# Eight of a tile's 32 column blocks go from VectorE to ScalarE, in one stage of a decode block's forward and backward pass

## The chip, the cores and the metric

The kernel runs on one core of a Trainium2 chip. That core has five engines, each with an instruction queue of its own that is worked in order: TensorE (PE in the profile, its weight loads PEld), VectorE (DVE), ScalarE (ACT), GpSimd (POOL) and SyncE (SP). Transfers are issued from the queues of SP, POOL and ACT and are carried by 16 DMA engines. The metric is the time of one execution on the device in microseconds (us), the median of several runs.

## The reference

A block of a transformer for one decoded token: layer norm, attention over a cache of 4096 keys and values, a residual, layer norm, a two-layer MLP with ReLU, a residual. The batch B is 2, there are H = 32 heads of 128, and the model width D is 640. The kernel computes the output and the gradients for x, the key and value caches, and the four weight matrices.

```
q      = layernorm(x) @ wq
scores = q . k * 128**-0.5 ;  p = softmax(scores) ;  o = p . v        # per batch and head
h      = x + o @ wo
out    = h + relu(layernorm(h) @ w1) @ w2
grads  = vjp of out for (x, k_cache, v_cache, wq, wo, w1, w2)
```

What costs most is the two caches, 2 x 32 x 4096 x 128 in bf16 each (1 MB for a head of a batch), which are read, and their gradients of the same size, which are written. For one batch and head, with `go` the gradient of the head's output, the gradient of V is the outer product of p and `go`; that of K is the outer product of the scores' gradient p * (V . go - const) and q.

## The kernel before, in words

A head's tile of a cache lies in SBUF as 128 partitions x 32 column blocks of 128: partition p holds rows 32p to 32p + 31 of the sequence, one in each block. gV and gK have the same layout. The kernel writes its engines' instructions in an order fixed by hand (a manual schedule); python generators that are stepped in turn decide which instruction is written when.

**First pass** (`p1_iter`): for each of the 64 pairs of batch and head, scores, softmax weights (`P_bf`), and sums that the output and the gradient of q need. **Second pass** (`p2_iter`): for each pair, the products of V with `go`, then gV and gK. The plan runs the first pass of the first batch, then the rest of the first pass with second-pass turns between, and from the loop's index 66 on the second pass alone (`i is None`). The order of the second pass is `turns`; turns 0 to 31 are batch 0, 32 to 63 batch 1. Turns 14 to 64 run in the stage where the second pass is alone.

One turn j of `p2_iter`, in the order in which it is written:

1. PE does the last quarter of turn j - 1's matvec (L436, `pair_matvec` with T3); VectorE makes `gsp` of it (L821), the column factor for gK.
2. PE spreads two rows (L830); ScalarE scales them into `rb` (L835): columns 0 to 127 are the row factor of gV, 128 to 255 that of gK. POOL copies a column of `P_bf` doubled into `pp` (L837), the column factor of gV.
3. PE transposes the first quarter of the V tile (`Wt`) into one of two PSUM banks (L423), and ScalarE copies it out to `t_sb` (L428). VectorE makes gK of turn j - 1 in two halves (L808) and POOL issues its store (L846).
4. The other three quarters are transposed and copied out in the same way (T1, T2, T3), each matvec one step behind. After T3's transposes the V tile's buffer is given back, which lets SP issue a later load.
5. VectorE makes gV of turn j in two halves of 16 blocks (L808, called from `outer_half`), and POOL issues its store (L865).

Between these steps background generators are stepped, whose instructions land in the same queues: the middle of the layer (`middle_gen`: layer norms, the MLP, and the products with w1 and wo, L644 on VectorE), the outer products of the weights' gradients (`fin_gen`, with ScalarE copies `ot` at L908 and `wide`, `ar` and the like), and the gradient of x (`gx_gen`). `fin_gen` starts within turns 22 and 23.

gV and gK tiles take 1 MB buffers from a list with the tag `g` (five of them in this stage), and V tiles from one with the tag `ld`. A buffer of `g` is free again when its store has landed, so the engine that first writes the next tile in it waits for that landing.

Of the kernel before, what the change touches and what calls it, by code (L numbers as in the profile page):

```python
# [7 lines left out]
FP32 = mybir.dt.float32  # L8
BF16 = mybir.dt.bfloat16
ALU = mybir.AluOpType  # L10
ACT = mybir.ActivationFunctionType
# [4 lines left out]
def kernel(  # L16
# [20 lines left out]
    nc = tc.nc  # L37

    B, Sq, D = A_x.shape
    _, H, Sk, Dh = A_k_cache.shape  # L40
# [4 lines left out]
    NSC = Sk // 128  # L45
# [7 lines left out]
    HALF = NSC // 2  # L53
# [13 lines left out]
    small = ctx.enter_context(tc.tile_pool(name="small", bufs=3))  # L67
# [136 lines left out]
    P_bf = cols.tile([128, B * H, NSC], BF16)  # L204
# [210 lines left out]
    def pair_transpose(nat, g, dve=False, busy=0):  # L415


        t_ps = pst([128, GT // 2, 128], FP32, "tps", "t_ps")
        warm(t_ps[:].rearrange("p j k -> p (j k)"), nat, g, busy)
        natf = nat[:].bitcast(FP32)  # L420
        for j in range(GT // 2):
            cc = (g * GT) // 2 + j
            nc.tensor.transpose(t_ps[:, j, :], natf[:, 2 * cc:2 * cc + 2, :].rearrange("p c k -> p (c k)"), ident_f[:])  # L423
        t_sb = mats.tile([128, GT // 2, 128], FP32, tag="XT", bufs=5, name="t_sb")
        if dve:
            nc.vector.tensor_copy(out=t_sb[:], in_=t_ps[:])  # L426
        else:
            nc.scalar.copy(out=t_sb[:], in_=t_ps[:])  # L428
        return t_sb
# [373 lines left out]
    def pairs_view(t):  # L803
        return t.rearrange("p s (a two) -> p s a two", two=2)

    def outer_half(dst, row, colp, k):
        sl = slice(k * HALF, (k + 1) * HALF)
        nc.vector.tensor_tensor(  # L808
            out=pairs_view(dst[:, sl, :]),
            in0=row.rearrange("p (a two) -> p a two", two=2)[:, None, :, :].to_broadcast([128, HALF, 64, 2]),  # L810
            in1=colp[:, sl, None, :].to_broadcast([128, HALF, 64, 2]), op=ALU.mult)

    def p2_iter(j, busy):

        c = S2[j] if j < NP1 else None
        p = S2[j - 1] if j >= 1 else None
        if p is not None:
            bp, hp = turns[j - 1]
            pair_matvec(p["dp"], p.pop("T3"), 3, gom[:, hp, bp, :, :])
            gsp = small.tile([128, NSC, 2], BF16, tag="gsp", name="gsp")  # L820
            nc.vector.scalar_tensor_tensor(  # L821
                out=gsp[:], in0=p["dp"][:, :, None].to_broadcast([128, NSC, 2]), scalar=negdot[:, hp, bp:bp + 1],
                in1=P_bf[:, bp * H + hp, :, None].to_broadcast([128, NSC, 2]), op0=ALU.add, op1=ALU.mult)
        if c is not None:
            b, h = turns[j]
            go = gom[:, h, b, :, :]

            bank = pst([128, 512], FP32, "sps", "dp_ps")
            for k, col in enumerate((goc, qsc)):
                nc.tensor.matmul(bank[:, 128 + k * 128:256 + k * 128],  # L830
                                 lhsT=col[:, h, b:b + 1].to_broadcast([128, 128]), rhs=ident_bf[:],
                                 start=True, stop=True)
            c["dp"] = bank[:, 0:NSC]
            rb = mats.tile([128, 256], BF16, tag="rb", bufs=4, name="rb")
            nc.scalar.activation(out=rb[:], in_=bank[:, 128:384], func=ACT.Copy, scale=rt[:, b, h:h + 1])  # L835
            pp = small.tile([128, NSC, 2], BF16, tag="pp", name="pp")
            nc.gpsimd.tensor_copy(out=pp[:], in_=P_bf[:, b * H + h, :, None].to_broadcast([128, NSC, 2]))  # L837
            c.update(rb=rb, pp=pp)
            c["T0"] = pair_transpose(c["W"], 0, busy=busy)
        if p is not None:  # L840
            gK = take("g", [128, NSC, 128], "gK")
            outer_half(gK, p["rb"][:, 128:256], gsp, 0)
        yield
        if p is not None:
            outer_half(gK, p["rb"][:, 128:256], gsp, 1)
            nc.gpsimd.dma_start(out=natural(out_2, bp, hp), in_=gK[:])  # L846
            give(gK)
            del S2[j - 1]
        yield
        if c is None:  # L850
            return
        c["T1"] = pair_transpose(c["W"], 1, busy=busy)
        pair_matvec(c["dp"], c.pop("T0"), 0, go)
        yield
        c["T2"] = pair_transpose(c["W"], 2, busy=busy)
        pair_matvec(c["dp"], c.pop("T1"), 1, go)
        yield
        c["T3"] = pair_transpose(c["W"], 3, busy=busy)
        give(c["W"], "g" if j < H and j != 1 and owned["g"] < 3 else None)
        pair_matvec(c["dp"], c.pop("T2"), 2, go)  # L860
        gV = take("g", [128, NSC, 128], "gV")
        outer_half(gV, c["rb"][:, 0:128], c["pp"], 0)
        yield
        outer_half(gV, c["rb"][:, 0:128], c["pp"], 1)
        nc.gpsimd.dma_start(out=natural(out_3, b, h), in_=gV[:])  # L865
        give(gV)
        yield
# [213 lines left out]
    i = j = 0  # L1081
# [46 lines left out]
    g2 = None  # L1128
# [11 lines left out]
    for n, (i, j) in enumerate(plan):  # L1140
        all_go = all(("go", B - 1, h) in done for h in range(H))
        if i is None and plan[n - 1][0] is not None:
            pkp.release()
            big1 = tc.alloc_tile_pool(name="big1", bufs=1)
            for _ in range(2):
                more_home("ld", big1)
            share(ld=KEPT[1] + 4, g=5)
        if all_go and not late[0]:
            wop.release()
            big3 = tc.alloc_tile_pool(name="big3", bufs=1, side="right")  # L1150
            for tag in ("ld", "g", "g", "q", "q", "q"):
                more_home(tag, big3)
        late[0] = all_go
        more = int(late[0])
        if fin is not None and not bg2 and not bg3:
            share(ld=8 + 3 * more, g=7 + 3 * more)
        elif fin is not None and j >= H + KEPT[1] - 1:
            share(ld=5 + more, g=5 + 2 * more, f=3, q=2 + 3 * more)
        if j is not None:
            while g2 is not None:  # L1160
                p2_step()
            if j < NP1:
                bg_until(("go", *turns[j]))
            g2 = p2_iter(j, 0)
        if i is None and ("w1", 1) in done and fin is None:
            wts.release()
            fin = tc.alloc_tile_pool(name="fin", bufs=1)
            big2 = tc.alloc_tile_pool(name="big2", bufs=1)
            more_home("f", big2)
            banks.update(sps=[2, 3], o=[4, 5, 6])  # L1170
            bg2.append(("fin", fin_gen(fin)))
            bg3.append(("gx", gx_gen(fin)))
        if i == 12:
            bg.append(("ga", ga_gen()))
        if i == H + 2:
            banks["bc"].insert(0, banks["sps"].pop(0))
        elif i == P2_AT:
            banks["bc"].remove(7)
            banks["sps"].insert(0, banks["bc"][0])
            banks["bc"] = [7]  # L1180
        rate = RATES[0 if i is not None and i <= H + 1 else 1 if j is None and i < P2_AT else
                     2 if i is not None else 3 if j <= H else 4]
        if i is None:
            spread[0] = 2
            at_k[0] = 1
            k = 0
            while g2 is not None:
                p2_step()
                pump()
                slot[0] = int(k in ((1, 3, 5) if j <= H else (1, 4)))  # L1190
                k += 1
                bg_step(0, rate)
                bg_step(1, RATE2)
                bg_step(2, RATE3)
            continue
        at = MIXED if j is not None else REST
        for k, _ in enumerate(p1_iter(i, i < H + 1, 0)):
            for _ in range(at.get(k, 0)):
                if g2 is not None:
                    p2_step()  # L1200
            if k == 5:
                a_heads(i)
            pump()

            spread[0] = 1 if i < P2_AT else 2
            at_k[0] = k
            if i >= P2_AT:
                slot[0] = int(k == 6 or (k == 1 and j is None))
            elif i > H + 1:
                slot[0] = {1: 2, 3: 1, 4: 1, 6: 1}.get(k, 0)  # L1210
            else:
                slot[0] = int(k in (1, 6))
            bg_step(0, rate)
            bg_step(1, 0.0)
        if i is not None and i in (H + 1, NP1 + 1):
            bg.append((f"m{i // H - 1}", middle_gen(i // H - 1)))
# [41 lines left out]
```

## Time and profile before

| what | before |
|---|---|
| median of 3 runs | 903.56 us (903.27 to 903.65) |
| the profiled execution | 902.98 us, of which the span of instructions is 901.1 |
| PE, PEld busy | 739.2 us (82%), 618.0 us (69%) |
| DVE busy | 695.8 us (77%) |
| ACT busy | 442.9 us (49%) |
| POOL busy | 192.9 us (21%) |
| moved | 362.87 MB, 403 GB/s over the span |
| mean granted TensorE clock | 0.775 of full speed |

Busy time is summed over the whole span, and stages differ: a mean says little of one stage, which is why the prediction asks for windows. In the groups of instructions a line names its source line, engine, operation, output and input tiles with shapes and count, then busy time in us and the mean of one in ns, then idle time of that engine just before, with what ended it. In the chain of waits each piece has a start, a length and what the end of the span hung on at that time.

The stores of gV are issued by POOL at 483.74 us (turn 14), 519.00 (19), 552.28 (23), 586.48 (28) and 622.37 (32).

### The profile page before, as it was taken

The numbers are of one execution on the slowest core, as the hardware profiler recorded it, in microseconds if no ns is written. First come the engines' busy times: TensorE is split into PE (matmuls) and PEld (weight loads), VectorE is DVE, ScalarE is ACT, GpSimd is POOL, SyncE is SP. The second block draws the span as 40 slices with busy tenths as digits, with TensorE's granted clock in tenths as the row PEclk, the third lists the DMA queues.
The fourth block names the chain that finished last, engine by engine and source line by source line (L and its number), as shares of the span: only waits on it lengthen the run. The fifth ranks groups of instructions, "written<-read, shape, count | busy, mean of one in ns | idle before, by whom it ended". The sixth has DMA issues, their size and how long they took to land.

```text
span 901.1 us, 24395 instructions
## 1 busy us (share of the span) xinstructions
PE 739.2 (82%) x10145; PEld 618.0 (69%) x10145; DVE 695.8 (77%) x1284; ACT 442.9 (49%) x1090; POOL 192.9 (21%) x330
## 2 busy tenths in 40 slices
PE   4998899899999897997877856865887799679780
PEld 4887788788888786886766845653766576466460
DVE  2665778677779886886878879978897459999972
ACT  1443334344456564564543534543665666467560
POOL 1343434343311111010011112111221111111120
PEclk9999999899999999898995556655566555575565
DMA  9999999999789999999999999999999999999997
GB/s 377 419 409 405 409 397 409 419 419 359 301 323 341 415 423 422 421 423 422 417 384 403 421 424 395 423 418 416 415 417 406 408 379 424 425 425 425 425 423 319
DMA packets 56430, 362.87 MB, mean 403 GB/s; under 512 B 5696, under 2 KB 11776, under 8 KB 15488
## 3 DMA queue, kind: packets, MB, share of 16 engines
q1 hardware_dynamic: 34664, 212.17, 58.3%
q0 software_dynamic: 18432, 134.23, 35.7%
q10 hardware_dynamic: 3224, 14.92, 4.0%
q8 instruction: 80, 1.31, 0.6%
q14 instruction: 30, 0.25, 0.1%
HBM read 212.16 MB, written 149.13 MB: 401 GB/s over the span
## 4 chain that ended last, share of the span: by engine, by line
PE 47%; DMA 25%; DVE 15%; ACT 5%; issue 5%; SPq 0%; POOL 0%; ACTq 0%; POOLq 0%; DVEq 0%
PE t_ps L423 20%; DMA Vt<-in_A_v_cache_dram 12%; PE m_ps L457 10%; DMA out_dram<-gV 7%; DVE gV L808 5%; DMA out_dram<-gK 4%; PE s_ps L436 3%; DVE gK L808 3%; PE u_ps L486 3%; ACT t_sb L428 3%; PE o_ps L902 3%; PE dp_ps L436 2%; DVE pk L464 2%; DVE junk L644 2%; DMA Kt<-in_A_k_cache_dram 2%
## 5 line engine op out<-in xcount | busy, mean ns | idle before, releaser
L428 ACT COPY t_sb<-t_ps 128x512 f32<-128x512 f32 x479 | 274.4, 587 | 212.5 <-PE t_ps L423 206.3
L436 PEld LDWEIGHTS <-t_sb 128*128 128x128 bf16 x4096 | 179.3, 102 | 43.1 <-ACT t_sb L428 21.4
L423 PE MATMUL t_ps<-ident_f,Wt 128*128 128x128 f32 x848 | 196.4, 380 | 0.2 <-ACT t_sb L428 0.2
L457 PE MATMUL m_ps<-pk,Vt 128*128 128x129 bf16 x2048 | 173.5, 224 | 18.0 <-DMA Vt<-in_A_v_cache_dram 16.0
L464 DVE TENSOR_TENSOR pk<-Kt,ep 128x2048 bf16<-128x2048 bf16 x128 | 156.5, 1223 | 30.8 <-ACT ep L512 14.1
L808 DVE TENSOR_TENSOR gK<-rb,gsp 128x2048 bf16<-128x2048 bf16 x128 | 152.5, 1225 | 17.2 <-DMA out_dram<-gV 15.2
L423 PE MATMUL t_ps<-ident_f,Kt 128*128 128x128 f32 x1024 | 156.9, 287 | 6.7 <-DMA Kt<-in_A_k_cache_dram 6.2
L808 DVE TENSOR_TENSOR gV<-rb,pp 128x2048 bf16<-128x2048 bf16 x128 | 152.9, 1219 | 10.0 <-DMA out_dram<-gK 7.9
L457 PEld LDWEIGHTS <-Vt 128*128 128x128 bf16 x2048 | 126.7, 99 | 49.2 <-issue 29.8
L423 PEld LDWEIGHTS t_ps<-ident_f,Wt 128*128 128x128 f32 x848 | 137.2, 198 | 29.3 <-issue 23.4
L423 PEld LDWEIGHTS t_ps<-ident_f,Kt 128*128 128x128 f32 x1024 | 114.0, 146 | 11.0 <-issue 5.9
L474 POOL COPY pk<-ep 128x16 bf16<-128x16 bf16 x80 | 84.8, 1062 | 166.5 <-ACT ep L512 86.8
L436 PE MATMUL dp_ps<-gom,t_sb 128*128 128x2 bf16 x2048 | 95.8, 168 | 10.9 <-ACT t_sb L428 10.4
L846 POOL DMA_DIRECT2D out_dram<-gK x64 | 34.0, 532 | 267.3 <-DVE gK L808 204.8
L865 POOL DMA_DIRECT2D out_dram<-gV x64 | 34.2, 534 | 258.1 <-DVE gV L808 202.2
L436 PE MATMUL s_ps<-qm,t_sb 128*128 128x2 bf16 x2048 | 87.7, 164 | 1.5 <-DVE t_sb L426 1.5
L908 ACT CAST ot<-o_ps 128x512 bf16<-128x512 f32 (+3 forms) x152 | 67.2, 492 | 10.7 <-DMA out_dram<-ot 9.2
L571 ACT CAST MT<-m_ps 128x128 bf16<-128x128 f32 x64 | 17.1, 267 | 107.7 <-PE m_ps L457 107.6
L821 DVE SCALAR_TENSOR_TENSOR gsp<-dp_ps,negdot,P_bf 128x64 bf16<-128x64 f32 x64 | 18.0, 281 | 52.0 <-PE dp_ps L436 51.6
L835 ACT ACTIVATE rb<-dp_ps,rt 128x256 bf16<-128x256 f32 x64 | 30.4, 475 | 56.0 <-PE dp_ps L830 55.2
L644 DVE CUSTOM_DVE_ANT_0 junk<-wo_t,hbc 128x640 bf16<-128x640 bf16 x64 | 52.4, 819 | 0.2
L644 DVE CUSTOM_DVE_ANT_0 gxj<-wqs,gqr 128x1024 bf16<-128x1024 bf16 x40 | 48.8, 1221 | 0.2
(198 smaller groups left out, 702.7 us busy)
## 6 DMA issues: line engine op xcount, KB each, us to landing
Kt<-in_A_k_cache_dram SPq DMA_DIRECT2D x64, 1024.0 KB, 15.0
Vt<-in_A_v_cache_dram SPq DMA_DIRECT2D x64, 1024.0 KB, 13.8
out_dram<-gV POOLq DMA_DIRECT2D x64, 1024.0 KB, 14.8
out_dram<-gK POOLq DMA_DIRECT2D x64, 1024.0 KB, 14.1
Wt<-in_A_v_cache_dram SPq DMA_DIRECT2D x53, 1024.0 KB, 12.5
wq_t<-in_A_wq_dram SPq DMA_DIRECT2D x5, 1024.0 KB, 6.9
wo_t<-in_A_wo_dram SPq DMA_DIRECT2D x4, 1280.0 KB
wqs<-in_A_wq_dram SPq DMA_DIRECT2D x5, 1024.0 KB, 15.8
```

The lines of the kernel that those rows point to most:

```text
L423: nc.tensor.transpose(t_ps[:, j, :], natf[:, 2 * cc:2 * cc + 2, :].rearrange("p c k -> p (c k)"), ident_f[:])
L428: nc.scalar.copy(out=t_sb[:], in_=t_ps[:])
L436: nc.tensor.matmul(dst[:, sc:sc + 2], lhsT=v[:, j, :, par], rhs=vecs[:, par, :], start=(par == 0), stop=(par == 1))
L457: nc.tensor.matmul(r["m"][:, 0:129], lhsT=r["V"][:, sc, :], rhs=r["pk"][sc // HALF][:, sc % HALF, 0:129], start=(sc == 0), stop=(sc == NSC ...
L464: nc.vector.tensor_tensor(out=p["pk"][k][:, :, 0:128].rearrange("p s (a two) -> p s a two", two=2), in0=p["K"][:, sl, :].rearrange("p s (a ...
L474: nc.gpsimd.tensor_copy(out=col, in_=e)
L644: nc.vector.tensor_tensor_reduce(out=junk[0:kc, 0:width], in0=in0, in1=in1, scale=1.0, scalar=0.0, op0=ALU.mult, op1=ALU.add, accum_out=acc)
L808: nc.vector.tensor_tensor(out=pairs_view(dst[:, sl, :]), in0=row.rearrange("p (a two) -> p a two", two=2)[:, None, :, :].to_broadcast([128 ...
L835: nc.scalar.activation(out=rb[:], in_=bank[:, 128:384], func=ACT.Copy, scale=rt[:, b, h:h + 1])
L846: nc.gpsimd.dma_start(out=natural(out_2, bp, hp), in_=gK[:])
L865: nc.gpsimd.dma_start(out=natural(out_3, b, h), in_=gV[:])
L908: nc.scalar.copy(out=ot[0:P, k, n0:n0 + nn], in_=o_ps[0:P, 0:nn])
```

## The change

In turns 14 to 32 (`i is None and j <= H`) VectorE writes only blocks 16 to 23 in the second half of gV. Blocks 24 to 31 are written by ScalarE, one activation each: the row factor of gV (`rb`, 128 columns) times one column of the weights as the activation's scale. That scale has to be in fp32, so POOL makes `pa`, a copy of the last eight columns of `P_bf` for the head. The eight activations stand on ScalarE's queue behind T3's copy of the same turn and ahead of the next turn's `rb`. The store of gV waits for both engines. Turns 0 to 13 and 33 to 63 keep the old form.

```diff
-    def outer_half(dst, row, colp, k):
-        sl = slice(k * HALF, (k + 1) * HALF)
+    def outer_half(dst, row, colp, k, short=0):
+        n = HALF - short
+        sl = slice(k * HALF, k * HALF + n)
         nc.vector.tensor_tensor(
             out=pairs_view(dst[:, sl, :]),
-            in0=row.rearrange("p (a two) -> p a two", two=2)[:, None, :, :].to_broadcast([128, HALF, 64, 2]),
-            in1=colp[:, sl, None, :].to_broadcast([128, HALF, 64, 2]), op=ALU.mult)
+            in0=row.rearrange("p (a two) -> p a two", two=2)[:, None, :, :].to_broadcast([128, n, 64, 2]),
+            in1=colp[:, sl, None, :].to_broadcast([128, n, 64, 2]), op=ALU.mult)
 
-    def p2_iter(j, busy):
+    def p2_iter(j, busy, act=0):
...
             c.update(rb=rb, pp=pp)
+            if act:
+                pa = small.tile([128, act], FP32, tag="pa", bufs=2, name="pa")
+                nc.gpsimd.tensor_copy(out=pa[:], in_=P_bf[:, b * H + h, NSC - act:NSC])
             c["T0"] = pair_transpose(c["W"], 0, busy=busy)
...
         outer_half(gV, c["rb"][:, 0:128], c["pp"], 0)
         yield
-        outer_half(gV, c["rb"][:, 0:128], c["pp"], 1)
+        outer_half(gV, c["rb"][:, 0:128], c["pp"], 1, act)
+        for k in range(act):
+            nc.scalar.activation(out=gV[:, NSC - act + k, :], in_=c["rb"][:, 0:128], func=ACT.Copy, scale=pa[:, k:k + 1])
         nc.gpsimd.dma_start(out=natural(out_3, b, h), in_=gV[:])
...
-            g2 = p2_iter(j, 0)
+            g2 = p2_iter(j, 0, 8 if i is None and j <= H else 0)
```

## The prediction

> **What bounds the kernel now.** I read the page's slices first (the two lines below are the mean busy share of the 16 DMA engines and what they moved, in 40 slices of 22.5 us), then found the stage. The stores of gV on POOL count the tiles: the 15th (turn 14) is issued at 483.74 us, the 33rd (turn 32) at 622.37, so the changed stage lies at about 478 to 624 us, 19 tiles in 146 us, 7.7 us a tile.
>
> ```profile
> DMA  9999999999789999999999999999999999999997
> GB/s 377 419 409 405 409 397 409 419 419 359 301 323 341 415 423 422 421 423 422 417 384 403 421 424 395 423 418 416 415 417 406 408 379 424 425 425 425 425 423 319
> ```
>
> The DMA engines are busy nearly everywhere and no long slice moves more than 425 GB/s. So the next view is busy time by engine in four stretches of the stage (columns: window, length, busy us and count of PE, weight load, DVE, ACT, POOL, granted clock, DMA share, GB/s).
>
> ```profile
> 478.00:503.00 25.00, 22.79 (x295) 20.85 (x293) 22.84 (x50) 11.74 (x21) 5.35 (x11) 0.57 1.01 402
> 503.00:548.00 45.00, 28.86 (x289) 26.06 (x289) 37.67 (x63) 16.66 (x31) 6.88 (x17) 0.50 1.01 425
> 548.00:582.00 34.00, 28.96 (x317) 23.50 (x315) 33.27 (x57) 21.69 (x53) 7.01 (x15) 0.66 1.00 404
> 582.00:624.00 42.00, 30.81 (x284) 23.85 (x284) 33.78 (x60) 20.85 (x47) 7.47 (x15) 0.53 1.01 419
> ```
>
> Two stretches run at 425 and 419: there transfers set the pace. Two run at 402 and 404, with VectorE busy 91% and 98% and PE 91% and 85% of the time. All the stage could gain is the missing bandwidth: 60.49 MB at 425 GB/s are 142.3 us, 3.7 us less than the 146.
>
> Who waits for whom in 478 to 624 us (total us, times, longest):
>
> ```profile
> ACT t_sb L428 <- PE t_ps L423: 55.1, 60, 14.6
> ACT rb L835 <- PE dp_ps L830: 13.5, 17, 1.4
> DVE gK L808 <- DMA out_dram<-gV: 9.3, 9, 1.9
> DVE gV L808 <- DMA out_dram<-gK: 4.9, 6, 1.7
> ```
>
> VectorE waits 14.2 us for stores to land and give a buffer back. ScalarE waits for PE, never for a store of gV or gK: today it can run ahead of VectorE. The chain of waits shows what that is worth, first in the 402 stretch and then behind it:
>
> ```profile
> 482.58 0.59 ACT t_sb L428
> 483.22 0.37 PE dp_ps L436 x8
> 483.59 0.24 PE dp_ps L830 x2
> 483.83 1.71 PE t_ps L423 x8
> ...
> 488.40 0.59 ACT t_sb L428
> ...
> 517.49 1.23 DVE gV L808
> ...
> 519.00 19.25 DMA out_dram<-gV
> ```
>
> From 479 to 516 us the chain is PE, ScalarE, PE: transpose, evacuate (L428), matvec. VectorE is on it only at the end, then a store's landing. PE, at half clock, sets the 402 stretch.
>
> **The change part by part.** Prices come from these groups of the stage (columns: count, busy us, mean ns; then idle before):
>
> ```profile
> L808 DVE TENSOR_TENSOR gV<-rb,pp 128x2048 bf16<-128x2048 bf16 x38 | 45.0, 1221 | 6.5 <-DMA out_dram<-gK 4.9 <-ACT ot L908 1.1 <-ACT t_sb L428 0.5
> L428 ACT COPY t_sb<-t_ps 128x512 f32<-128x512 f32 x84 | 49.0, 587 | 58.5 <-PE t_ps L423 57.2 <-ACT ot L908 0.4 <-PE pr_ps L339 0.4
> L835 ACT ACTIVATE rb<-dp_ps,rt 128x256 bf16<-128x256 f32 x22 | 10.4, 475 | 13.8 <-PE dp_ps L830 13.8
> L885 ACT CAST gr<-rw_ps 128x128 bf16<-128x128 f32 x1 | 0.3, 271 | 0.0
> ```
>
> *Removed from VectorE.* The second half of gV shrinks from 2048 to 1024 columns, 19 times. It saves 0.61 us if the cost is all columns, and at least (1221 - 280) / 2 = 0.47 us if as much as the whole 280 ns of the small gsp operation (L821, 128x64) is fixed cost. I take 0.55, nearer the proportional end: 10.4 us of VectorE time in all.
>
> *Added to ScalarE.* 8 activations of 128x128 a tile, 152 in all, each with a column as its scale. No row has one reading SBUF at that width; the nearest is rb (475 ns, 256 wide, a column as its scale). Evacuations fall from 587 to 271 ns between 512 and 128 columns, 0.82 ns a column, so 128 columns make 475 - 105 = 370 ns. Two evacuations in a row take 1.07 us in place of 1.17, so 0.10 overlaps: 8 x 0.27 + 0.1 = 2.3 us. Ends: 1.5 us by the plain 271 ns row with that overlap, 3.8 us at eight times rb without any. I take 2.3, because rb has the same form: 43 us over the stage, on an engine that is busy 71 of 146.
>
> The Trainium skill ("ScalarE: Activation LUTs", the section on what ACT_TABLE_LOAD costs) gives 186 ns + 0.833 ns an element + 93 ns for a pointer operand, and 93 ns of overlap. That makes 386 ns alone, an estimate of 2.4 us for the eight, and agrees with the rb row (492 against 475 ns). The same page's rules for kernel authors say to multiply on VectorE rather than ScalarE; by it the swap gives 0.55 us for 2.4 us and pays only where ScalarE is really idle.
>
> *Added to POOL.* 19 copies of 128x8 (pa) behind pp. The pp copies, eight times wider, take 0.25 to 1.3 us; I take 0.25. Nothing waits: POOL idles 1.4 us or more ahead of nearly every gK store. Without that cover a store would leave at most 1.3 us later. PE and SP keep their order of instructions.
>
> *Waits added.* (1) The store of gV now waits for ScalarE also. Behind it on POOL stand pp and pa of the next turn and the store of gK. They do not suffer: gK needs gsp, which needs the matvec of the same T3 evacuation that ScalarE does just before its eight; gsp and two halves of gK (0.28 + 2.36 us) end after the eight (2.3). (2) The first activation waits for the gV buffer, that is, for a store to land. Behind it on ScalarE's queue are the next rb, the next four evacuations, the background's copies (fbc, hbc, wide, ot) and the issues of ot stores. PE waits for all these through its PSUM banks. So PE's lead over VectorE (turn 22's last evacuation begins at 529.25, its gV at 542.11: 12.9 us) shrinks to about one turn.
>
> *On the path, turns 14 to 18.* PE can do matvec 3, the two row matmuls and T0 and T1 of the next turn (0.4 + 0.25 + 2.1 = 2.8 us at half clock) beside the eight. But rb (0.48) and T0's evacuation (0.59) then come behind them: 2.3 + 0.48 + 0.59 = 3.4 us to the next matvec instead of 2.8, so 0.6 a turn, up to 1 where rb was early; the turn grows from 6.1 us (rb 483.86 to 508.19 is four turns) to 6.8. That is still under the 7.4 us that 3.15 MB a turn take at 425 GB/s, so only the start costs. T3 of turn 14 is evacuated by 483.2, so its store leaves at about 485.6 instead of 483.74. The packet records show the store queue empty from 486.1 to 486.9 there, and 328 GB/s in 484 to 488. A further 1.7 us with loads alone, at some 290 of 425 GB/s (what 550 to 554 us moves, where the queue is empty again), costs +0.6 us (ends 0 and 1.7).
>
> *Turns 23 to 28 (548 to 582).* Here the background's copies lie on ScalarE too. From rb to the end of the fourth evacuation took 7.2, 3.4, 6.5, 6.3 and 3.3 us in turns 24 to 28, mean 5.3; with 2.3 and 0.1 of hand-over a turn is 7.7 us, where gV stores leave every 6.84 us today: up to 4.3 us late over five turns. The store queue covers part: a store begins 4.3 to 7.5 us after its issue here, against about 2.7 on an empty queue. I leave 2.3 us uncovered, with a third still filled by loads: +1.5 us (ends 0 and 4.3).
>
> *Behind the stage.* Stores issued at 663.86 and 667.32 begin 3.2 and 2.5 us later: the queue is down to bare latency, so lead that PE and the store queue lost before is not made up. Some +0.9 us (0 to 3).
>
> *Gain kept.* VectorE's 10.4 us count only where VectorE and no landing or PE held a gK: part of 484 to 488 and 548 to 556 (345 GB/s). One tile's 0.55: -0.6 (ends -3.7 and 0).
>
> Sum: +0.6 + 1.5 + 0.9 - 0.6 = +2.4 us on the profiled run's 902.98 us (span 901.1, 1.9 around it). That run is 0.6 under the median of 903.56, so 906.0 against the median.
>
> **The rivals.**
> *A, no change within 0.2%* (1.8 us, about what a measurement here can tell from nothing): the bytes set the time. For it: 425 and 419 GB/s in 87 of 146 us, and stores that wait 4 us or more in queue. Then late turns are swallowed and only +0.6 and -0.6 remain: 903.6.
> *B, faster:* ScalarE tied to the buffers stops PE from running ahead. Today it takes its W tiles early and stands 13.4 us in one wait at csum (L217, for lb_mm), with no load in the packet records from 540 to 548; then 548 to 556 moves 345 GB/s. If loads spread evenly and VectorE is 0.55 lighter, both dips fill: 2.5 to 3.7 us, 900.5. It decides if the eight take no more than the 1.5 us of the low end, for a turn with background copies is then 5.3 + 1.5 + 0.1 = 6.9 us, as today. Against it: in the first dip the chain is on PE and ScalarE, and VectorE isn't on it.
> *C, much slower:* the eight cost 3.8 us, a turn with background copies is 9.2 us, above the 8.4 that a turn takes in the transfer-bound 582 to 624 (five turns in 42 us); over the ten turns 23 to 32 that is +8 us, 911.6. It decides once ScalarE's turn passes 8.4 us, that is, from eights of 3.0 us on. Against it: two evacuations in a row do overlap.
>
> **How the numbers follow.** My sum (1.8 to 5 us slower) 0.34, A 0.34, B 0.22, C 0.10. Slower is my sum and C, 0.44; same 0.34; faster 0.22. The forecast is 906.0, own range 905.4 to 908.6. The 8-in-10 range leaves out half of B (0.11, below its middle gain of 2.7 us: 900.9) and most of C (0.07, above 909.9).
>
> **What would show it.** gV's second half at about 0.67 us; eight activations in 2.3 us; the wait of ScalarE for a store's landing new on the list; rb of turn 22 near 536 instead of 525; stores of gV behind ScalarE in turns 14 to 17 and 24 to 27; GB/s of 484 to 490 under 328 and of 556 to 585 under 420. The prediction is wrong if the 548 to 556 dip goes and 556 to 585 stays at 420, or if eight activations take far from 2.3 us.

## The result, and the profile after

The changed kernel took 898.96 us, median of 22 runs (895.05 to 905.23), against 903.26 us for the kernel before, also of 22 runs (899.17 to 907.45). The ratio is 0.9953, with a 95% interval of 0.9937 to 0.9969: faster by some 4.3 us. The forecast was 906.0 with a range of 900.9 to 909.9, so sign and range were both wrong. The single runs of the two kernels spread by 0.9% and 1.1%, far more than the three runs shown at first let suppose, so a pair of profiles alone proves little.

The profiled execution took 895.05 us, its span is 893.3. Slices of 22.3 us, as before:

```profile
DMA  9999999999889999999999999999999999999996
GB/s 378 425 419 417 416 408 417 426 423 367 314 322 357 424 424 425 424 423 425 420 406 394 420 422 416 411 415 421 416 424 415 408 386 425 425 425 424 427 422 294
```

The reader should look at the slices that nobody had looked at: the first nine. All nine move more than before, by 1 to 12 GB/s, and they end more than 260 us ahead of the first changed instruction (`pa`, at 466.98 us). They hold the first pass of the first batch, which only loads. Below are windows of 50 to 200 us, first the kernel before, then the changed one (window, length, busy us and count of PE, weight load, DVE, ACT, POOL, clock, DMA share, GB/s):

```profile
50.00:200.00 150.00, 140.42 (x2355) 122.32 (x2353) 110.11 (x206) 57.94 (x178) 60.55 (x75) 0.95 1.02 409
```

```profile
50.00:200.00 150.00, 146.04 (x2483) 128.24 (x2482) 114.56 (x214) 61.16 (x186) 64.01 (x79) 0.97 1.02 418
```

The program's instructions are the same here and stand in the same order, the DMA share is 1.02 in both, and 2% more bytes arrive. PE's waits for loads in this window shrink with it, again before and then after:

```profile
L457 PE MATMUL m_ps<-pk,Vt 128*128 128x129 bf16 x792 | 66.8, 225 | 6.0 <-DMA Vt<-in_A_v_cache_dram 6.0
L423 PE MATMUL t_ps<-ident_f,Kt 128*128 128x128 f32 x397 | 59.2, 283 | 3.6 <-DMA Kt<-in_A_k_cache_dram 3.4
```

```profile
L457 PE MATMUL m_ps<-pk,Vt 128*128 128x129 bf16 x848 | 70.5, 223 | 2.7 <-DMA Vt<-in_A_v_cache_dram 2.6
L423 PE MATMUL t_ps<-ident_f,Kt 128*128 128x128 f32 x416 | 61.9, 283 | 1.2 <-DMA Kt<-in_A_k_cache_dram 1.2
```

The store of turn 13's gV, the last ahead of the changed stage, leaves at 466.27 us in place of 473.94. So 7.7 of the 7.9 us between this pair of profiles are there before the change begins.

In the stage itself everything that was to happen happened. The changed stage lies 8 us earlier now, so its four stretches are 470 to 616:

```profile
470.00:495.00 25.00, 22.09 (x275) 20.33 (x275) 21.15 (x50) 15.86 (x41) 5.91 (x13) 0.50 0.99 397
495.00:540.00 45.00, 33.12 (x340) 29.17 (x339) 37.62 (x70) 32.41 (x86) 14.29 (x24) 0.50 1.01 421
540.00:574.00 34.00, 25.65 (x244) 20.36 (x242) 25.91 (x48) 26.68 (x76) 8.61 (x16) 0.60 1.01 416
574.00:616.00 42.00, 32.73 (x293) 25.44 (x294) 34.93 (x65) 32.12 (x89) 11.95 (x20) 0.50 1.01 416
```

VectorE's busy time falls from 127.6 to 119.6 us and ScalarE's rises from 71.0 to 107.1. The rates were 402, 425, 404 and 419 before: the third stretch gains 12 GB/s, the three others lose 3 to 5. The instructions of gV (duration min/median/max in ns), and the waits in 470 to 616:

```profile
L870 ACT ACTIVATE gV<-rb,pa x152: 384/388/423, 475.6 to 615.3; 128x128 bf16<-128x128 bf16 x152
L809 DVE TENSOR_TENSOR gV<-rb,pp x128: 678/1217/1227, 264.3 to 873.2; 128x2048 bf16<-128x2048 bf16 x109, 128x1024 bf16<-128x1024 bf16 x19
```

```profile
POOL out_dram L871 <- ACT gV L870: 71.8, 16, 6.7
ACT t_sb L428 <- PE t_ps L423: 38.8, 43, 9.9
DVE gsp L822 <- PE dp_ps L436: 13.6, 6, 4.0
...
DVE gV L809 <- DMA out_dram<-gK: 2.9, 5, 1.0
DVE gK L809 <- DMA out_dram<-gV: 2.6, 3, 1.8
ACT gV L870 <- DMA out_dram<-gK: 2.5, 3, 1.5
```

VectorE's waits for landings fall from 14.2 to 5.5 us, and it now waits 13.6 us for PE, which it did not before.

### The profile page after: what moved, and what is told of

Same layout as the page of the kernel before. It is cut to its first block, busy times and chain, and to the rows that moved or that the text cites. A ratio compares the mean times of both kernels' runs of the same rounds, so it can differ in the third digit from the quotient of the medians.

```text
span 893.3 us, 24580 instructions
## 1 busy us (share of the span) xinstructions
PE 742.4 (83%) x10145; PEld 619.6 (69%) x10145; DVE 686.8 (77%) x1284; ACT 482.9 (54%) x1242; POOL 208.0 (23%) x349
## 4 chain that ended last, share of the span: by engine, by line
PE 45%; DMA 26%; DVE 12%; ACT 9%; issue 4%; SPq 0%; POOL 0%; ACTq 0%; POOLq 0%; DVEq 0%
PE t_ps L423 19%; DMA Vt<-in_A_v_cache_dram 11%; PE m_ps L457 10%; DMA out_dram<-gV 7%; DMA out_dram<-gK 5%; PE s_ps L436 3%; ACT gV L870 3%; DVE gV L809 3%; PE u_ps L486 3%; ACT t_sb L428 3%; DMA wqs<-in_A_wq_dram 3%; PE o_ps L908 2%; PE dp_ps L436 2%; DVE gK L809 2%; DVE pk L464 2%
## 5 line engine op out<-in xcount | busy, mean ns | idle before, releaser
L423 PE MATMUL t_ps<-ident_f,Wt 128*128 128x128 f32 x848 | 198.8, 384 | 0.2 <-ACT t_sb L428 0.2
L457 PE MATMUL m_ps<-pk,Vt 128*128 128x129 bf16 x2048 | 172.5, 223 | 12.9 <-DMA Vt<-in_A_v_cache_dram 11.4
L464 DVE TENSOR_TENSOR pk<-Kt,ep 128x2048 bf16<-128x2048 bf16 x128 | 156.4, 1223 | 30.1 <-ACT ep L512 14.2
L423 PEld LDWEIGHTS t_ps<-ident_f,Wt 128*128 128x128 f32 x848 | 139.0, 200 | 25.2 <-issue 18.0
L809 DVE TENSOR_TENSOR gV<-rb,pp 128x2048 bf16<-128x2048 bf16 (+1 forms) x128 | 142.6, 1139 | 8.1 <-DMA out_dram<-gK 7.8
## 6 DMA issues: line engine op xcount, KB each, us to landing
out_dram<-gK POOLq DMA_DIRECT2D x64, 1024.0 KB, 14.2
Wt<-in_A_v_cache_dram SPq DMA_DIRECT2D x53, 1024.0 KB, 12.9
```

Of the source, the lines that this page charges most:

```text
L457: nc.tensor.matmul(r["m"][:, 0:129], lhsT=r["V"][:, sc, :], rhs=r["pk"][sc // HALF][:, sc % HALF, 0:129], start=(sc == 0), stop=(sc == NSC ...
L464: nc.vector.tensor_tensor(out=p["pk"][k][:, :, 0:128].rearrange("p s (a two) -> p s a two", two=2), in0=p["K"][:, sl, :].rearrange("p s (a ...
L809: nc.vector.tensor_tensor(out=pairs_view(dst[:, sl, :]), in0=row.rearrange("p (a two) -> p a two", two=2)[:, None, :, :].to_broadcast([128 ...
```

## The experiments

What, if not the swap, comes with the change? The tile `pa` takes 2 x 32 bytes of every SBUF partition. The pools lie one behind another, so all that is allocated behind it moves up by 64 bytes: `t_sb`, `rb`, and the 1 MB buffers. The program's list of addresses shows these buffers at 47552 + 8192 n before and at 47616 + 8192 n in the changed kernel. 47552 is 192 above a multiple of 256; 47616 is a multiple of 512. Theory S says that the gain is made in the stage, theory L that the addresses make it. Each ratio below is against runs of the kernel before that were taken beside that experiment: their medians were 904.20 us (34 runs) for the first four experiments, 904.46 (32) for the next four and 901.87 (18) for the last four.

**The changed kernel again.**

> The changed kernel once more, unaltered, with a second profile. In the first pair of profiles the changed kernel was already 7.7 us ahead when the store of turn 13's gV left (466.3 against 473.9 us), before any changed instruction had run, and took 1.3 us more from there to the store of turn 32 (149.8 against 148.4). Theory S (the gain is made inside the changed stage): ratio about 0.995 again, and the time from turn 13's store to turn 33's is 2 to 4 us under the 156.9 us of before. Theory N (the median's gain is mostly spread between executions): ratio 0.998 to 1.002, and stage times within 1.5 us of before's.

898.63 us (12 runs), ratio 0.9947 (0.9927 to 0.9967). The median's gain is real, which fells theory N. From turn 13's store to turn 33's it took 153.3 us here, so the stage alone let S stand.

**POOL's copies without the swap.**

```diff
-        outer_half(gV, c["rb"][:, 0:128], c["pp"], 1, act)
-        for k in range(act):
+        outer_half(gV, c["rb"][:, 0:128], c["pp"], 1)
+        for k in range(0):
```

> Keeps the tile pa and POOL's 19 copies, but VectorE makes all of gV again and ScalarE's activations are left out. It has the new layout of SBUF and the new POOL instructions without the swap. Theory S: 1.000 (within 0.2%). Rival L (layout, or anything else that comes with the tile and not with the swap, makes the gain, all over the kernel): 0.995, and stores as early at turn 13 as in the changed kernel.

898.23 us (12 runs), ratio 0.9937 (0.9910 to 0.9964): the whole gain, with no block moved to ScalarE. Theory S is out. The second sign of L was met only in part: turn 13's store left at 471.52 us, 2.4 us ahead of before's, while the changed kernel's two profiles have 466.27 and 469.31.

**One block in place of eight.**

```diff
-            g2 = p2_iter(j, 0, 8 if i is None and j <= H else 0)
+            g2 = p2_iter(j, 0, 1 if i is None and j <= H else 0)
```

> ScalarE makes one block of 32 in place of eight, VectorE the other 31. ScalarE is tied to gV's buffer as in the changed kernel, for about 0.4 us a tile, and VectorE is relieved by only some 0.07 us. If the tie is what gains (PE no longer runs ahead, loads spread, the prediction's rival B): 0.995 or below, 2 to 4 us less in the stage. If VectorE's lighter load gains: 0.999 to 1.000. If the eight cost something and the tie gains: below 0.995.

898.98 us (12 runs), ratio 0.9939 (0.9917 to 0.9961). Beside the run before it this shows nothing for the tie: all the runs so far in which `pa` has a place of its own lie at 898 to 899. My expectation had not allowed for the address in this run, and read alone it would have spoken for the tie.

**VectorE's relief alone.**

```diff
-        for k in range(act):
+        for k in range(0):
...
+        if act:
+            nc.gpsimd.memset(gV[:, NSC - act:, :], 0.0)
         nc.gpsimd.dma_start(out=natural(out_3, b, h), in_=gV[:])
```

> VectorE leaves out eight blocks as in the changed kernel, but ScalarE does nothing for them: POOL sets them to zero ahead of the store, so these eight blocks of gV are not computed. ScalarE may run ahead as before. If VectorE's relief is the gain: 0.995 or below. If the tie is the gain: 0.998 to 1.000. The prediction had 0.6 us for the relief, 0.9993.

898.08 us (11 runs), ratio 0.9938 (0.9917 to 0.9960): again the level of the runs with `pa`. Taking the 10 us off VectorE, with POOL's memsets of 1 us a tile in their place and nothing added to ScalarE, gives no more than the tile alone.

**64 bytes and nothing else.** This is the kernel before, with a tile that nobody reads:

```diff
+    padp = ctx.enter_context(tc.tile_pool(name="padp", bufs=1))
+    pad = padp.tile([128, 16], FP32, name="pad")
+    nc.gpsimd.memset(pad[:], 0.0)
     mats = ctx.enter_context(tc.tile_pool(name="mats", bufs=1))
```

> The kernel before with nothing of the change: only an unused tile of 64 bytes a partition ahead of the pools of t_sb, rb and the 1 MB buffers, which moves the left-hand 1 MB buffers from byte 47552 of a partition (64 more than a multiple of 128) to 47616 (a multiple of 512), as the changed kernel's pa tile does. Theory L (the address makes the gain): 0.994, 4 to 6 us less, with loads at 415 GB/s or more in 50 to 150 us where before had 406. Rival P (POOL's copies, or the altered program, make it): 1.000.

896.37 us (9 runs), ratio 0.9913 (0.9885 to 0.9941). Window 50 to 200 us of its profile:

```profile
50.00:200.00 150.00, 144.19 (x2475) 126.37 (x2474) 113.78 (x212) 61.20 (x185) 62.33 (x78) 0.98 1.02 418
```

The same 418 GB/s as the changed kernel. Theory L holds and P falls, though 8.1 us under the 904.46 taken beside it is more than the 4 to 6 expected.

**The swap without the move.** `pa` lies in the slot of a tile that is used only at the start. It has one slot here instead of two, which adds no wait: POOL writes it behind the store that waits for the eight activations.

```diff
-                pa = small.tile([128, act], FP32, tag="pa", bufs=2, name="pa")
-                nc.gpsimd.tensor_copy(out=pa[:], in_=P_bf[:, b * H + h, NSC - act:NSC])
+                pa = small.tile([128, 32], FP32, tag="zero", bufs=1, name="pa")
+                nc.gpsimd.tensor_copy(out=pa[:, 0:act], in_=P_bf[:, b * H + h, NSC - act:NSC])
```

> The whole change, with pa laid into the 128 bytes of a tile that is used only at the start, so that every other tile keeps the address it has in the kernel before. Theory L: the swap itself, apart from the address, is worth about what the changed kernel has over the run with POOL's copies alone, 898.7 against 898.2, so 1.000 to 1.001. Theory S (the swap gains): 0.995. The prediction's sum: 1.0027.

903.01 us (12 runs), ratio 0.9993 (0.9969 to 1.0017): -0.6 us, with -2.8 to +1.5 as its interval. This is the price of what the prediction was about. The two windows below are the loads of its first pass and its stage (478 to 624):

```profile
50.00:200.00 150.00, 141.78 (x2376) 123.69 (x2375) 110.52 (x209) 59.33 (x182) 60.77 (x77) 0.95 1.02 409
```

```profile
478.00:624.00 146.00, 113.30 (x1138) 95.00 (x1135) 117.54 (x227) 106.82 (x290) 37.57 (x73) 0.52 1.01 412
```

409 GB/s in the first pass, as before. In the stage VectorE has 10.0 us less to do and ScalarE 36 more, and DMA moves 412 GB/s where it moved 414.

**Which multiple counts.** Three runs move the left-hand 1 MB buffers of the kernel before down. 128 bytes come free when the tile `zero` shares the slots of `gsp`, 256 when `xr` shares those of `rb`; the 64 bytes of the padded run then go on top, or not.

```diff
-        zero = small.tile([128, H * B], BF16, tag="zero", bufs=1, name="zero")
+        zero = small.tile([128, NSC, 2], BF16, tag="gsp", name="zero")[:].rearrange("p a b -> p (a b)")
...
-    xr = cols.tile([4 * ND, 128], BF16)
+    xr = mats.tile([128, 256], BF16, tag="rb", bufs=4, name="xr")[0:4 * ND, 0:128]
```

> The kernel before with its left-hand 1 MB buffers 128 bytes lower (byte 47424, again 64 more than a multiple of 128), by putting a tile that is used once at the start into the slots of another. If being a multiple of 128 is what counts: 1.000, although the addresses moved. If any move gains, or the number that counts is larger than 128 in some other way: not 1.000.

903.71 us (12 runs), ratio 0.9981 (0.9956 to 1.0005), 409 GB/s in 50 to 200 us: moving the buffers does nothing by itself that is clear of noise.

> As the run 128 bytes lower, with the tile of 64 bytes of the padded run besides: byte 47488, a multiple of 128 but not of 256 or 512. If 128 counts: 0.994, like the padded run. If 256 or 512 counts: 1.000, or between.

903.36 us (12 runs), ratio 0.9975 (0.9949 to 1.0001), 410 GB/s: a multiple of 128 does not do it. This run has the padded run's extra tile and its memset too, so these did not make the padded run's gain.

> The kernel before with its left-hand 1 MB buffers 192 bytes lower, at byte 47360, a multiple of 256 but not of 512. If 256 is what counts: 415 GB/s or more in 50 to 150 us and 0.992 to 0.995, like the padded run. If 512 counts: 407 GB/s and 0.998, like the runs 64 and 128 bytes lower. The Trainium skill (DMA: Bandwidth & Descriptors, how a descriptor splits into AXI transactions) says 256: a descriptor that starts off a 256-byte boundary begins with a part-used transaction.

897.05 us (6 runs), ratio 0.9927 (0.9904 to 0.9950). Windows 50 to 200, first 64 bytes down (a multiple of 128), then 192 down (a multiple of 256):

```profile
50.00:200.00 150.00, 140.03 (x2375) 122.56 (x2373) 110.65 (x208) 59.25 (x180) 60.75 (x75) 0.98 1.02 410
```

```profile
50.00:200.00 150.00, 142.49 (x2464) 124.71 (x2462) 113.63 (x213) 60.45 (x185) 62.35 (x78) 0.99 1.02 417
```

So a multiple of 256 is enough, and 64, 128 and 192 above one cost about the same. The rates carry this; the intervals of the times just touch (0.9949 to 1.0001 at 64 down, 0.9904 to 0.9950 at 192 down).

**The buffers alone.** The 64 bytes stand behind the pool of `t_sb` and `rb`:

```diff
+    padp = ctx.enter_context(tc.tile_pool(name="padp", bufs=1))
+    pad = padp.tile([128, 16], FP32, name="pad")
+    nc.gpsimd.memset(pad[:], 0.0)
     big = ctx.enter_context(tc.tile_pool(name="big", bufs=1))
```

> The padded run with the 64 bytes behind the pool of t_sb and rb, so that these keep their addresses and only the left-hand 1 MB buffers move to a multiple of 512. If the gain is that of transfers into and out of these buffers: 0.992 to 0.995. If it is that of engines' accesses to t_sb and rb: 1.000.

897.40 us (9 runs), ratio 0.9949 (0.9926 to 0.9972), 417 GB/s. It is the buffers, not `t_sb` and `rb`. Small tiles behind the buffers move with them (`pk`, say), but the loads do not touch these.

**All 1 MB buffers on a multiple of 512, without and with the swap.** Both move the right-hand pools down by 480 bytes as well; room comes from sharing the slots named above and those of `ln_sq` and `ln_cent` with two tiles of the backward layer norm.

```diff
+    rpad = ctx.enter_context(tc.tile_pool(name="rpad", bufs=1, side="right"))
+    rp = rpad.tile([128, 120], FP32, name="rp")
+    nc.gpsimd.memset(rp[:], 0.0)
     wop = tc.alloc_tile_pool(name="wop", bufs=1, side="right")
```

> The kernel before, with all 1 MB buffers at multiples of 512, those at the right-hand end too (they stood 32 bytes below one); room comes from putting three small tiles of the start and the end into slots of others. If the address counts for every transfer, another tenth of the stores and the 5 MB of wo gain: 0.2 to 1 us under the padded run, 0.990 to 0.993. If stores do not gain: as the padded run.

896.20 us (8 runs), ratio 0.9927 (0.9900 to 0.9953). 50 to 200 us moves 419 GB/s, one or two more than the padded run's 418 and 417; the total can't be told from it.

> All 1 MB buffers at multiples of 512, and the swap of the change on top. If the swap is worth nothing: the same as the run without the swap, within 2 us. If it gains where transfers no longer hold VectorE back: lower. The prediction's own sum, +2.4 us for the swap, would show here as 2 us or more above.

897.07 us (8 runs), ratio 0.9941 (0.9918 to 0.9965). With and without the swap lie 0.9 us apart, inside the intervals: the swap is worth nothing here either.

## Why the prediction was wrong

**The step that failed** is "Added to POOL". It costed `pa` as 19 copies, found that nothing waits for them, and so at nothing. That was right for the copies. It left out that `pa` is also 64 bytes of SBUF, and that other tiles stand behind it; the move of these tiles alone took 8.1 us off (the padded run, 896.37 against 904.46). I followed the order of instructions on each engine and not the addresses, although both are in the built program. All the profiles fall into two groups, by the address of the left-hand buffers:

| left-hand 1 MB buffers start at | profiles | GB/s in 50 to 200 us | first gV store (turn 0) leaves at |
|---|---|---|---|
| 64, 128 or 192 above a multiple of 256 | 4 | 409.0 to 409.7 | 269.7 to 273.8, mean 272.6 us |
| a multiple of 256 | 10 | 416.9 to 419.3 | 266.9 to 270.8, mean 268.3 us |

The means are 4.3 us apart at the first store, and the medians of the first result differ by as much. The spans of the 14 profiles are further apart, 902.0 us in the mean of the first group and 895.4 in that of the second: two thirds of these 6.6 us are there at the first store. The other 2.3 us arise mostly from turn 13's store to turn 33's (157.7 us in the mean of the first group and 155.5 in that of the second, 153.3 to 158.8 in single profiles); whether they come from the addresses or are scatter is open. From the first store to turn 13's it took 200.7 and 199.8 us, and 750 to 850 us moves 424 to 425 GB/s in all 14. Over whole executions the ratios of the second group lie between 0.9913 and 0.9953, so the gain is 4 to 8 us and known no better than that.

The packet records show the loss where it arises. In 50 to 200 us a load's packet of 8192 bytes took 316.5 to 317.4 ns in the mean in the four profiles of the first group, and 311.2 to 312.1 in the ten of the second; in 750 to 850 us it took 309.5 to 310.1 in both. Why the address matters to loads alone and not in the mix of loads and stores was not tried.

**The swap, by the prediction's own terms.** Their sum was +2.4 us; the run without the move gave -0.6 (-2.8 to +1.5). Rival A, no change, was the right case for the swap, and all that the sum had above it came from two terms, the +1.5 us of turns 23 to 28 and the +0.9 us behind the stage.

- *VectorE's saving, 0.55 us a tile*: the half op takes 678 ns at the least against 1217, so 0.54. Right.
- *The eight activations, 2.3 us*: turn 14's ran from 475.62 to 478.06, so 2.44, with 388 ns for one in the median. The row-based value was 6% low. The 386 ns by the Trainium skill ("ScalarE: Activation LUTs", the section on what ACT_TABLE_LOAD costs) and the estimate of 2.4 us from them agree with the trace. The page's rule to multiply on VectorE decided nothing here: 36 us more on ScalarE and 10 less on VectorE left the time as it was.
- *PE loses its lead*: right. It was 12.9 us at its largest in the profile before (turn 22, and 14.8 to 19.6 in the seven others with VectorE's full halves); with the eight activations it is 0.9 to 2.6 in four profiles.
- *Turns 14 to 18 grow from 6.1 to 6.8 us*: 7.05 (rb of turn 15 at 477.97, of turn 19 at 506.17). Turn 14's store leaves 12.1 us behind turn 13's instead of 9.8. The packet records show the store queue empty for 1.5 and 1.8 us there instead of once for 0.85, and the stretch moves 397 GB/s instead of 402 (396 in the run without the move). The term of +0.6 us had the right sign and twice the size: 5 in 402 of 25 us is 0.3.
- *Turns 23 to 28, +1.5 us*: this term failed. The turns did get slower, more than thought (stores of turns 23 and 28 at 542.17 and 583.34: 8.2 us each, against 7.7 forecast and 6.84 before; 8.2 to 8.4 in all four profiles with the eight). But the transfers of the stretch did not suffer by it: they moved 416 GB/s instead of 404, and 415 in the run without the move. Before, VectorE and PE hurried through these turns after a jam (8.3 us a turn from 19 to 23), and in between loads had stopped for 10 us (539.1 to 549.5) and the store queue was empty for 0.8; now turns 19 to 23 take 7.2, and the dip to 345 is gone. That part of rival B came true, but it gained nothing that lasts: the three other stretches lost 3 to 5 GB/s, and 404 was the lowest of the eight profiles without the eight activations, whose seven others moved 407 to 425 from 548 to 582.
- *Behind the stage, +0.9 us*: it fits in sign, not clear of scatter. From turn 13's store to turn 33's took 155.0 us in the mean of four profiles with the eight (153.3 to 157.7) and 156.7 in eight without (153.7 to 158.8). From turn 33's to turn 63's it was 254.9 (253.8 to 256.1) against 252.6 (250.9 to 254.8). So in the means the stage is 1.7 us shorter and the rest 2.3 longer. The ranges overlap, and three of the four with the eight are on a multiple of 256 against five of the eight without; at before's addresses the stage took 157.7 us with the eight and 156.8 to 158.8 in the three profiles without. A gain in the stage is not shown. What fits the longer rest is that with PE tied to the stores 21.0 to 21.5 MB are loaded between turn 13's store and turn 33's instead of 21.4 to 22.7, and the remainder must be loaded later. The rate between the two stores is 412 to 416 GB/s with the eight and 414 to 418 without, so a store that leaves earlier here shows a changed order of the bytes and not a faster kernel.

**Rival B** had the sign, and its 900.5 was 1.5 us above the measured median, but by luck: its mechanism shows in the stage and is worth nothing at the end. Its bound was drawn from the stage alone (3.7 us of missing bandwidth at most), and a gain made elsewhere is not held by that. The lower end of the forecast's range, 900.9, took 2.7 us as B's middle gain, though the 2.5 to 3.7 us given for B have their middle at 3.1, which is the 900.5; the measured 898.96 lies under both.

**The signs.** One was misread: 328 GB/s is the rate of 484 to 488 us, and 484 to 490 moved 354 in the profile before. In the run without the move these windows moved 379 and 392, so that sign did not come. The other did: 556 to 585 moved 413 there, under 420, where before had 422.

## What to carry to other kernels

A change that adds a tile, however small, moves what is allocated behind it: compare the addresses of the buffers that DMA fills, besides the order of instructions, and when a profile differs ahead of the first changed instruction, look there first. Test an edit apart from its layout, by giving its tile a place that moves nothing, and test the layout apart from the edit. In this stage, where DMA moved 412 to 418 GB/s with and without the swap, moving 10 us of work from one engine to another changed the order of the bytes and not the end, so an earlier store in the middle of a run is no gain by itself.

The 64 bytes without the swap (896.4 us) and all buffers on multiples of 512 (896.2) are the fastest medians. Both beat the kernel before (0.9913 and 0.9927); against the changed kernel the intervals overlap.

## What the runs showed of the hardware that was not expected

In 50 to 200 us, which is mostly loads of 8 KB a partition from HBM into SBUF, DMA moved 409 to 410 GB/s where the buffers start 64, 128 or 192 bytes above a multiple of 256, and at 417 to 419 where they start on one: some 2% in a stretch of loads alone. One packet of 8192 bytes took 317 ns against 312. In the mixed stretch of 750 to 850 us no profile showed the difference.

The Trainium skill ("DMA: Bandwidth & Descriptors", how a descriptor splits into AXI transactions) says that a descriptor that starts off a 256-byte boundary begins with a transaction of which only a part is used. The page words this for reading, while in these loads SBUF is the side that is written. The runs agree on the 256. They do not show a price that grows with the distance, as a count of beats would give (an estimate from that page: 258, 260 and 262 beats for 8 KB in place of 256, for 64, 128 and 192 bytes); the three measured 409.5, 409.7 and 409.0 GB/s.
